# Three q, k turns of batch 2 by DMA transpose, an early gelu table, and a new order for batch 3's loads: a streaming-attention and gMLP kernel on one Trainium2 core

## The chip, the core and the metric

The kernel runs on one core of one Trainium2 chip. A time is device microseconds (us) of one execution; "the median" is over plain runs, and the profile is of one further execution, whose own time is given beside its span (first to last instruction of the program). The engines are named as in the profile: PE (TensorE), DVE (VectorE), ACT (ScalarE), POOL (GpSimd), SP (SyncE, which here only issues DMAs). Batches are counted from 0, so "batch 2" is the third and "batch 3" the fourth.

## The reference

Sliding-window attention with four sink tokens, then a gMLP block on the result. B = 4 batches, H = 8 heads, S = 768 tokens, head size 64; d_model = 512, d_ff = 1024.

```python
keep = is_sink | ((rel >= 0) & (rel < window))          # n_sink 4, window 128
a = softmax(where(keep, q @ k.T / sqrt(D), -1e9))
x = (a @ v).transpose(0, 2, 1, 3).reshape(B, S, 512)
h = gelu_tanh(x @ w_in)                                  # 512 -> 1024
u, v = h[..., :512], h[..., 512:]
v_n = (v - mean(v)) / sqrt(var(v) + 1e-6) * g_ln
v_s = einsum('ts,bsd->btd', w_sg, v_n) + b_sg[None, :, None]
out = x + (u * v_s) @ w_out
```

## The kernel before

All work is split into small steps, written by name in one long string, `STEPS` (from L20), and emitted in exactly that order. A step name is a function and its indices: `QK.2.0.1` is `QK(2, 0, 1)`. Each engine runs its own instructions in the order of the string, and each DMA is issued by the engine that owns its step: SP for transposes (`DQ`, `DK`, `XD`) and stores (`ST`), POOL for the loads that change f32 into bf16 (`LQ`, `LK`, `LVH`). So a step that waits holds back everything behind it on its engine, and the place of a step in the string sets its place in a queue.

For each batch the steps are these.

- `LQ`, `LK` (L225, L228) load 128 tokens of q or k, six each; `LVH` (L271) loads v for four heads, two each.
- q and k must stand with the head dimension on the partitions. For batches 0 to 2 this is done on PE: `TQ`, `TK` (`turns`, L361) put eight 128x128 transposes into one PSUM buffer, and `EQ`, `EK` (`turned`, L404; L197 and L198 are the copy itself) copy it to `qT`, `kT` on ACT (.A) or DVE (.D). For batch 3 it is done by `DQ`, `DK` (`by_dma`, L435), one DMA transpose on SP for the same eight blocks, with neither PE, PSUM nor a copy. One such step covers two tiles of 128 tokens: group 0, 1 or 2.
- `KS` takes the four sink keys, `SK` (L455) computes the sink scores of tokens 256 to 767 and `SX` (L462) their exponentials. `QK` computes window scores of a pair of heads p for two token tiles g, `EX` the exponentials (ACT), `MK` the masks (DVE or POOL), `AV` the product with v, `NR` the division.
- `XD` (L552) transposes the attention result by DMA, in two halves of three tiles. `MV` (L559, tiles 2g and 2g + 1) and `MU` (L600) are the first projection, `GV` (L566) and `GU` the gelu on ACT. `BN`, `RS` (L583, a power on POOL), `NM` and `Z` normalise.
- `SP` is the product over tokens (all six `Z` needed), `GT` and `GM` the gate, `OU` the second projection, `RA` the residual and `ST` the store.

PSUM is used through two rings: two wide buffers (`sc`) for `QK`, `MV` and `MU`, and four narrow ones (`mm`) for the rest. Two rings of two buffers hold `qT` and `kT`, so batch 2 writes where batch 0 was. The string overlaps batches: while the gate of batch b runs, attention of batch b + 1 or b + 2 runs between its steps. Exponentials and gelu need different tables on ACT; the first use of the other kind brings an ACT_TABLE_LOAD, which shows under the line of the activation that it serves.

The stretch that the change touches first: after the last exponentials of batch 2's group 0 (`EX.2.3.0`) and `OU.0.2`, PE does `TK.2.2`, `TQ.2.1`, `TQ.2.2`, then `MV.1.0`, `MU.1.0`, `MV.1.1`, `MV.1.2`, `MU.1.1`, `MU.1.2`, `OU.0.3`, `SK.2.0`, `QK.2.0.1`, `QK.2.1.1`, `OU.0.4`, `SP.1.0.0`. `MV.1.1` reuses the wide buffer of `MV.1.0`, which `GV.1.0` empties, and is the first to need the second half of `XD` (`XD.1.1`).

Of the kernel before, what the change touches and what calls it, by code (L numbers as in the profile page):

```python
# [28 lines left out]
MV.0.0 XE.0.1.A LK.1.2 NR.0.0.2 MK.0.3.2.D LK.1.3 NR.0.1.2 AV.0.2.2 AV.0.3.2 LQ.1.2 NR.0.2.2 GV.0.0 MV.0.1 NR.0.3.2
LQ.1.3 BN.0.0 LWS.1 XT.0.2 GV.0.1 MU.0.1 XE.0.2.A BN.0.1 WT.0 GU.0.1 TK.1.0 MV.0.2 RS.0.1 EK.1.0.A LK.1.4 NM.0.1  # L30
WE.0.A WT.1 GV.0.2 LK.1.5 TK.1.1 MU.0.2 LB.P EK.1.1.A BN.0.2 Z.0.0.A LK.2.0 WT.2 GU.0.2 MU.0.0 WE.1.D RS.0.2 WE.2.D
Z.0.1.A LQ.2.0 NM.0.2 Z.0.2.A Z.0.3.D Z.0.4.D WT.3 LQ.2.1 WT.4 GU.0.0 WE.3.D WT.5 LQ.1.4 Z.0.5.D TQ.1.1 QK.1.0.0
EQ.1.1.D QK.1.1.0 LQ.1.5 SP.0.0.0 WE.4.D LK.2.1 EX.1.0.0 VSM.1 SP.0.0.1 WE.5.D EX.1.1.0 LVH.1.0 GT.0.0.0 TK.1.2 KS.1
GT.0.0.1 QK.1.2.0 QK.1.3.0 EX.1.2.0 SP.0.0.2 LVH.1.1 GM.0.0.0.D EX.1.3.0 MK.1.2.0.D TQ.2.0 EK.1.2.A LQ.2.2 QK.1.0.1
EQ.2.0.D QK.1.1.1 TQ.1.2 EX.1.0.1 GT.0.0.2 LWO SP.0.0.3 EQ.1.2.D EX.1.1.1 LK.2.2 MK.1.0.1.D TK.2.0 MK.1.0.0.D QK.1.2.1
LK.2.3 EK.2.0.A QK.1.3.1 MK.1.3.0.D SK.1.0 GM.0.0.1.D LQ.2.3 SP.0.1.0 EX.1.2.1 GT.0.0.3 MK.1.1.0.D LQ.2.4 EX.1.3.1
SP.0.1.1 MK.1.1.1.D LQ.2.5 MK.1.2.1.D SX.1.0 QK.1.0.2 QK.1.1.2 GT.0.1.0 EX.1.0.2 GM.0.0.2.P SP.0.1.2 GT.0.1.1 EX.1.1.2
LK.2.4 GM.0.1.0.D AV.1.0.0 MK.1.3.1.D AV.1.1.0 LK.2.5 GM.0.0.3.D QK.1.2.2 GT.0.1.2 QK.1.3.2 EX.1.2.2 SP.0.1.3 NR.1.0.0
MK.1.1.2.P EX.1.3.2 NR.1.1.0 AV.1.2.0 AV.1.3.0 MK.1.0.2.P GT.0.1.3 QK.2.0.0 QK.2.1.0 NR.1.2.0 EX.2.0.0 OU.0.0
MK.1.2.2.P NR.1.3.0 TK.2.1 RA.0.0 AV.1.0.1 XD.1.0 EK.2.1.A MK.1.3.2.P AV.1.1.1 NR.1.0.1 AV.1.2.1 EX.2.1.0 GM.0.1.2.P  # L40
NR.1.1.1 AV.1.3.1 NR.1.2.1 QK.2.2.0 LK.3.0 QK.2.3.0 EX.2.2.0 OU.0.1 NR.1.3.1 GM.0.1.3.P EX.2.3.0 OU.0.2 XD.1.1 RA.0.1
GM.0.1.1.P TK.2.2 MK.2.3.0.D TQ.2.1 LVH.2.0 TQ.2.2 EQ.2.1.D MV.1.0 EQ.2.2.D LQ.3.0 EK.2.2.D LQ.3.1 VSM.2 MU.1.0 GV.1.0
MK.2.1.0.D LVH.2.1 BN.1.0 MV.1.1 GU.1.0 LQ.3.2 RA.0.2 LQ.3.3 MK.2.0.0.D MV.1.2 GV.1.1 MK.2.2.0.D LK.3.1 KS.2 LK.3.2
BN.1.1 MU.1.1 GV.1.2 LK.3.3 BN.1.2 RS.1.1 MU.1.2 GU.1.1 LQ.3.4 NM.1.1 Z.1.0.A RS.1.2 OU.0.3 GU.1.2 LQ.3.5 NM.1.2
Z.1.1.D SK.2.0 Z.1.4.D QK.2.0.1 Z.1.2.D Z.1.3.A QK.2.1.1 Z.1.5.D OU.0.4 RA.0.3 DK.3.0 SP.1.0.0 RA.0.4 SX.2.0 EX.2.0.1
SP.1.0.1 GT.1.0.0 DQ.3.0 EX.2.1.1 GM.1.0.0.D SP.1.1.0 MK.2.0.1.P GT.1.0.1 QK.2.2.1 ST.0.3 GT.1.1.0 QK.2.3.1 GM.1.0.1.P
DQ.3.1 EX.2.2.1 AV.2.0.0 SP.1.1.1 MK.2.1.1.D EX.2.3.1 MK.2.2.1.P NR.2.0.0 AV.2.1.0 QK.2.0.2 DQ.3.2 QK.2.1.2 KS.3
EX.2.0.2 MK.2.3.1.P NR.2.1.0 SP.1.1.2 GT.1.1.1 EX.2.1.2 OU.0.5 MK.2.0.2.P GT.1.1.2 ST.0.0 ST.0.4 QK.2.2.2 RA.0.5
QK.2.3.2 MK.2.1.2.P EX.2.2.2 AV.2.2.0 AV.2.3.0 NR.2.2.0 SP.1.1.3 EX.2.3.2 NR.2.3.0 QK.3.0.0 MK.2.3.2.P QK.3.1.0
GT.1.1.3 XD.2.0 EX.3.0.0 AV.2.0.1 MK.2.2.2.D AV.2.1.1 EX.3.1.0 NR.2.0.1 AV.2.2.1 GM.1.1.3.P ST.0.1 NR.2.1.1 AV.2.3.1  # L50
ST.0.2 ST.0.5 GM.1.1.0.P SK.3.0 NR.2.2.1 QK.3.2.0 QK.3.3.0 NR.2.3.1 EX.3.2.0 GM.1.1.2.P SP.1.0.2 EX.3.3.0 XD.2.1
SP.1.0.3 GT.1.0.2 SX.3.0 MK.3.3.0.D MV.2.0 GM.1.0.2.P DK.3.1 GM.1.1.1.D LK.3.4 MK.3.0.0.D OU.1.3 LVH.3.0 GV.2.0 OU.1.4
RA.1.3 LVH.3.1 OU.1.5 ST.1.3 RA.1.4 GT.1.0.3 MV.2.1 ST.1.4 MK.3.1.0.D LK.3.5 BN.2.0 GM.1.0.3.P MV.2.2 GV.2.1 BN.2.1
MU.2.1 GV.2.2 BN.2.2 RS.2.1 MU.2.0 GU.2.1 NM.2.1 RA.1.5 RS.2.2 MU.2.2 GU.2.0 NM.2.2 Z.2.4.D Z.2.5.D Z.2.0.A Z.2.1.D
OU.1.0 GU.2.2 Z.2.2.D MK.3.2.0.D OU.1.1 RA.1.0 Z.2.3.D QK.3.0.1 QK.3.1.1 RA.1.1 SP.2.0.0 EX.3.0.1 DK.3.2 EX.3.1.1
OU.1.2 MK.3.0.1.P GT.2.0.0 ST.1.5 VSM.3 ST.1.0 QK.3.2.1 ST.1.1 QK.3.3.1 EX.3.2.1 SP.2.1.0 GM.2.0.0.D MK.3.1.1.P RA.1.2
EX.3.3.1 SP.2.0.1 ST.1.2 MK.3.3.1.P QK.3.0.2 GT.2.0.1 QK.3.1.2 EX.3.0.2 SP.2.1.1 GT.2.1.0 MK.3.2.1.P EX.3.1.2
GM.2.1.0.D SP.2.1.2 GT.2.1.1 GM.2.0.1.D AV.3.0.0 MK.3.1.2.P GT.2.1.2 AV.3.1.0 NR.3.0.0 AV.3.2.0 AV.3.3.0 MK.3.0.2.P
NR.3.1.0 QK.3.2.2 QK.3.3.2 EX.3.2.2 SP.2.0.2 NR.3.2.0 NR.3.3.0 EX.3.3.2 SP.2.0.3 MK.3.2.2.P GT.2.0.2 XD.3.0 AV.3.0.1
GT.2.0.3 MK.3.3.2.P AV.3.1.1 NR.3.0.1 AV.3.2.1 GM.2.0.3.P NR.3.1.1 AV.3.3.1 SP.2.1.3 GM.2.0.2.D GM.2.1.1.P NR.3.2.1  # L60
OU.2.0 NR.3.3.1 GT.2.1.3 XD.3.1 OU.2.1 RA.2.0 GM.2.1.3.P OU.2.2 GM.2.1.2.D ST.2.0 RA.2.1 MV.3.0 RA.2.2 ST.2.1 OU.2.3
GV.3.0 OU.2.4 BN.3.0 MV.3.1 RA.2.3 RA.2.4 MV.3.2 ST.2.3 GV.3.1 ST.2.2 ST.2.4 BN.3.1 OU.2.5 GV.3.2 MU.3.2 BN.3.2 RS.3.1
MU.3.1 GU.3.2 NM.3.1 RS.3.2 NM.3.2 Z.3.0.D Z.3.1.A MU.3.0 Z.3.2.D Z.3.3.A Z.3.4.A Z.3.5.D RA.2.5 ST.2.5 SP.3.1.0
GU.3.0 SP.3.1.1 GU.3.1 GT.3.1.0 SP.3.1.2 GM.3.1.0.D GT.3.1.1 SP.3.1.3 GM.3.1.1.D GT.3.1.2 SP.3.0.0 GM.3.1.2.D SP.3.0.1
GT.3.0.0 GT.3.1.3 SP.3.0.2 GT.3.0.1 GM.3.1.3.P SP.3.0.3 GM.3.0.0.D GM.3.0.1.P GT.3.0.2 OU.3.3 GM.3.0.2.D GT.3.0.3
OU.3.4 GM.3.0.3.D RA.3.3 OU.3.0 RA.3.4 ST.3.3 OU.3.1 RA.3.0 ST.3.4 OU.3.2 ST.3.0 RA.3.1 OU.3.5 ST.3.1 RA.3.2 ST.3.2
RA.3.5 ST.3.5
"""


# [5 lines left out]
def kernel(  # L76
# [489 lines left out]
    def GV(b, g):  # L566
        return nc.scalar.activation(out=vt.new((b, g)), in_=sc_ring["v", b, g], func=AF.Gelu_apprx_tanh)  # L567
# [4 lines left out]
    def BN(b, g):
        mv = mvs.get(b)
        sts = [tiny.tile([128, 6], F32, name=f"st{jl}") for jl in range(2)]
        for jl in range(2):
            nc.vector.bn_stats(out=sts[jl], in_=vt[b, g][:, jl, :])  # L576
        for jl in range(2):
            nc.vector.bn_aggr(out=mv[:, 2 * g + jl, :], in_=sts[jl])
        if g:
            nc.vector.tensor_scalar(out=rs.get(b)[:, part(g)], in0=mv[:, part(g), 1], scalar1=1e-6,  # L580
                                    scalar2=None, op0=ALU.add)

    def RS(b, g):  # L583
        r = rs[b][:, part(g)]
        nc.gpsimd.tensor_tensor(r, r, neg_half[:, part(g)], op=ALU.pow)  # L585
# [127 lines left out]
```

## Time and profile before

| | |
|---|---|
| median of 3 runs | 157.62 us (157.57 to 157.83) |
| the profiled execution | 156.68 us, of it span 155.0 us |
| granted TensorE clock over the span | 0.997 |
| busy: PE / DVE / POOL / ACT | 93% / 79% / 64% / 64% of the span |
| DMA queue of POOL's loads (q0) | 64608 packets, 11.01 MB |
| DMA queue of SP's DMAs (q1) | 21544 packets, 13.41 MB |
| one DMA transpose of 128x1024 (`DQ`, `DK`), issue to landing | 3.0 to 4.4 us |
| eight PE transposes, start to start of one | 0.056 us |
| the copy of 128x1024 behind them on DVE | 0.68 us |
| ACT_TABLE_LOAD | 1.28 us |

How to read it: an engine's share is the mean over the span, and PE is the engine that is nearly always at work. A group's line gives its count, its busy time and the idle time before it with the one that ended that idle time. A timeline line gives start and length in us, engine, line, operation, out<-in, and in brackets the idle time of that engine just before. "PEld" is PE's weight load, which overlaps its matmuls. A q behind an engine's name marks its queue of DMA issues.

### The profile page before, as it was taken

Reading aid. Unit: us, or ns where it says so; the run is one execution under the profiler, and the core shown is the slowest. Engines: PE = TensorE matmul, PEld = TensorE weight load, DVE = VectorE, ACT = ScalarE, POOL = GpSimd, SP = SyncE. Lnnn points to the kernel's source line nnn. Section 1 sums busy time; section 2 is a strip of 40 time slices with the busy share of each in tenths; the row PEclk is TensorE's granted clock in tenths of the full one; section 3 lists DMA queues with packets and bytes.
Section 4 is the critical chain, followed back from the end, with each engine's and each line's share of the span. In section 5 each row is a group of like instructions: output and inputs, shape, how many; then the busy total and the mean of one; then the engine's idle time right before and its main releaser. Section 6 shows DMA issues by size and latency. Waiting matters only on the chain.

```text
span 155.0 us, 3736 instructions
## 1 busy us (share of the span) xinstructions
PE 144.0 (93%) x1483; PEld 93.5 (60%) x1495; DVE 122.9 (79%) x295; ACT 98.9 (64%) x110; POOL 99.9 (64%) x127
## 2 busy tenths in 40 slices
PE   6697799999999989989999999999999999999990
...
GB/s 162 261 367 162 149 194 210 166 194 218 147 149 153 181 159 135 153 152 156 153 255 138 140 270 179 177 190 80 217 68 24 82 237 4 203 68 2 0 237 171
DMA packets 86169, 24.65 MB, mean 159 GB/s; under 512 B 78660, under 2 KB 83016, under 8 KB 86152
## 3 DMA queue, kind: packets, MB, share of 16 engines
q0 software_dynamic: 64608, 11.01, 96.1%
q1 hardware_dynamic: 21544, 13.41, 33.6%
...
## 4 chain that ended last, share of the span: by engine, by line
PE 59%; DMA 15%; POOL 10%; DVE 7%; issue 4%; ACT 2%; SPq 1%; ACTq 0%; POOLq 0%
PE mm L624 15%; PE mm L641 12%; DMA v_sb<-in_v_dram 11%; PE sc L563 10%; PE sc L604 8%; PE sc L480 4%; DMA uT<-in_k_dram 4%; PE mm L521 3%; POOL q L223 3%; DVE st L576 2%; PE mm L525 2%; POOL P L495 2%; PE mm L528 2%; POOL P L498 2%; DVE P L492 1%
## 5 line engine op out<-in xcount | busy, mean ns | idle before, releaser
L485 ACT ACTIVATE P<-sc 128x1024 bf16<-128x1024 f32 (+1 forms) x48 | 43.5, 956 | 10.0 <-PE sc L480 9.9
L624 PE MATMUL mm<-wsgT,z 128*128 128x384 bf16 x192 | 34.1, 327 | 0.0
L624 PEld LDWEIGHTS <-z 128*128 128x128 bf16 x192 | 17.7, 98 | 11.9 <-issue 0.7
L563 PE MATMUL sc<-w_in_sb,xT 128*128 128x512 bf16 x92 | 21.8, 379 | 0.9 <-ACT vt L567 0.7
L629 DVE SCALAR_TENSOR_TENSOR gtmp<-mm,g_sb,b_bc 128x384 bf16<-128x384 f32 x32 | 19.2, 612 | 4.2 <-PE mm L624 3.6
L641 PE MATMUL mm<-w_out_sb,wsg_gated 128*128 128x512 bf16 x89 | 22.0, 379 | 0.3
L604 PE MATMUL sc<-xT,w_in_sb 128*128 128x256 bf16 x192 | 22.1, 273 | 0.0
L634 POOL TENSOR_TENSOR wsg_gated<-gtmp,uT 128x384 bf16<-128x384 bf16 x15 | 14.9, 1004 | 10.9 <-DVE gtmp L629 10.9
L576 DVE BATCH_NORM_STATS2 st<-vt 128x6 f32<-128x512 f32 x24 | 15.4, 685 | 7.5 <-ACT vt L567 7.4
L495 POOL TENSOR_SCALAR_AFFINE_SELECT P<-P 128x512 bf16<-128x512 bf16 x21 | 14.1, 669 | 11.3 <-ACT P L485 11.0
L604 PEld LDWEIGHTS <-w_in_sb 128*128 128x128 bf16 x192 | 18.6, 98 | 3.0
L538 DVE TENSOR_TENSOR x_sb<-mm,rcp 128x384 bf16<-128x384 f32 (+1 forms) x36 | 18.5, 513 | 1.2
L567 ACT ACTIVATE vt<-sc 128x1024 f32<-128x1024 f32 x12 | 12.3, 1028 | 9.0 <-PE sc L563 8.9
L645 DVE TENSOR_TENSOR ot<-mm,x_sb 128x512 f32<-128x512 f32 x24 | 16.1, 684 | 2.3 <-PE mm L641 2.2
L585 POOL TENSOR_TENSOR rs<-rs,neg_half 128x4 f32<-128x4 f32 (+1 forms) x8 | 7.0, 869 | 16.5 <-DVE rs L580 15.1
L223 POOL DMA_DIRECT2D k<-in_k_dram x18 | 16.4, 924 | 1.2 <-DMA v_sb<-in_v_dram 1.2
L521 PE MATMUL mm<-v_sb,P 128*128 128x65 bf16 x192 | 16.3, 194 | 0.7 <-DVE x_sb L538 0.4
L223 POOL DMA_DIRECT2D q<-in_q_dram x18 | 16.7, 949 | 0.0
L521 PEld LDWEIGHTS <-P 128*128 128x128 bf16 x192 | 14.6, 97 | 2.7 <-issue 0.6
L525 PE MATMUL mm<-v_sb,P 128*128 128x65 bf16 x160 | 15.5, 194 | 0.4 <-POOL P L498 0.4
L563 PEld LDWEIGHTS <-xT 128*128 128x128 bf16 x96 | 9.2, 98 | 10.9 <-issue 0.9
L480 PE MATMUL sc<-qT,kT 64*128 64x128 bf16 (+1 forms) x256 | 14.8, 238 | 1.0 <-DVE qT L198 0.6
...
## 6 DMA issues: line engine op xcount, KB each, us to landing
...
```

The source lines that it names most:

```text
L223: return nc.gpsimd.dma_start(out=dst.rearrange("p (h d) -> p h d", h=H), in_=heads(src, b, i))
L480: nc.tensor.matmul(sc[:, hl, c:c + 128 * ni], at(kT, b)[rows, j, p, :], at(qT, b)[rows, i:i + ni, p, :], start=not biased, stop=(not biase ...
L485: nc.scalar.activation(out=P.new((b, p, g))[:, :, 0:w], in_=sc_ring[b, p, g][:, :, 0:w], func=AF.Exp, scale=scale)
L521: nc.tensor.matmul(av[:, il, hl, :], pt[:, hl, c:c + 128], vb[:, h, i, :], start=first, stop=False)
L525: nc.tensor.matmul(av[:, il, hl, :], pt[:, hl, c:c + 128], vb[:, h, i - 1, :], start=False, stop=(i < 2 and il == n - 1 and hl == 1))
L538: nc.vector.tensor_mul(x_sb.get(b)[:, i0:i0 + n, 128 * p:128 * (p + 1)].rearrange("p t (h d) -> p t h d", h=2), av[:, :, :, 0:Dh], rcp[:, ...
L563: nc.tensor.matmul(hp[:, jl, :], xT[b][:, 2 * g + jl, c, :], w_in_sb[:, c, d_half:2 * d_half], start=(c == 0), stop=(c == KD - 1))
L576: nc.vector.bn_stats(out=sts[jl], in_=vt[b, g][:, jl, :])
L604: nc.tensor.matmul(hp[:, dc // 2, 256 * (dc % 2):256 * (dc % 2 + 1)], w_in_sb[:, c, 128 * dc:128 * (dc + 1)], xT[b][:, 2 * g:2 * g + 2, c, :],
L624: nc.tensor.matmul(ps[:, 0:NH], z[b][:, si, 128 * dc:128 * (dc + 1)], wsgT[:, si, NH * hf:NH * (hf + 1)], start=(si == 0), stop=(si == NT ...
L629: nc.vector.scalar_tensor_tensor(out=gtmp.new((b, hf, dc)), in0=mm_ring["g", b, hf, dc][:, 0:NH], scalar=g_sb[:, dc:dc + 1], in1=b_bc[:, N ...
L641: nc.tensor.matmul(ps, gated(b, hf)[:, dc, 128 * tl:128 * (tl + 1)], w_out_sb[:, dc, :], start=(dc == 0), stop=(dc == KU - 1))
```

## The change

Four edits, three of them in the string alone.

1. `TK.2.2`, `TQ.2.1`, `TQ.2.2` and their copies `EQ.2.1.D`, `EQ.2.2.D`, `EK.2.2.D` are taken out. `DQ.2.1`, `DQ.2.2`, `DK.2.2` are put in, on SP directly behind `XD.1.1`. Group 0 of q and groups 0 and 1 of k of batch 2 stay on PE.
2. A new step `TL`, one gelu of a 128x1 tile into an unused tile, stands on ACT between `EX.2.3.0` and `GV.1.0`.
3. On POOL, the loads of batch 3 are reordered: `LK.3.1` moves up ahead of `LVH.2.1`; `LK.3.2` and `LK.3.3` move from ahead of `RS.1.1` to behind `RS.1.2`, and `LQ.3.5` follows `RS.1.2` directly, ahead of them.
4. `SK.3.0` moves on PE from ahead of `QK.3.2.0` to behind `QK.3.1.1`, `SX.3.0` on ACT from behind `EX.3.3.0` to behind `EX.3.1.1`.

The lines of the string are broken anew in the diff, so it is shown here step by step, + and - at the places of the steps; the new function is whole.

```diff
 EX.2.3.0
+TL
 OU.0.2 XD.1.1
+DQ.2.1 DQ.2.2 DK.2.2
 RA.0.1 GM.0.1.1.P
-TK.2.2
 MK.2.3.0.D
-TQ.2.1
 LVH.2.0
-TQ.2.2 EQ.2.1.D
 MV.1.0
-EQ.2.2.D
 LQ.3.0
-EK.2.2.D
 LQ.3.1
+LK.3.1
 VSM.2 MU.1.0 GV.1.0 MK.2.1.0.D LVH.2.1 BN.1.0 MV.1.1 GU.1.0 LQ.3.2 RA.0.2 LQ.3.3 MK.2.0.0.D MV.1.2 GV.1.1 MK.2.2.0.D
-LK.3.1
 KS.2
-LK.3.2
 BN.1.1 MU.1.1 GV.1.2
-LK.3.3
 BN.1.2 RS.1.1
+LQ.3.4
 MU.1.2 GU.1.1
-LQ.3.4
 NM.1.1 Z.1.0.A RS.1.2
+LQ.3.5 LK.3.2 LK.3.3
 OU.0.3 GU.1.2
-LQ.3.5
 NM.1.2 Z.1.1.D SK.2.0
...
 GM.1.1.0.P
-SK.3.0
 NR.2.2.1 QK.3.2.0 QK.3.3.0 NR.2.3.1 EX.3.2.0 GM.1.1.2.P SP.1.0.2 EX.3.3.0 XD.2.1 SP.1.0.3 GT.1.0.2
-SX.3.0
 MK.3.3.0.D MV.2.0
...
 QK.3.0.1 QK.3.1.1
+SK.3.0
 RA.1.1 SP.2.0.0 EX.3.0.1 DK.3.2 EX.3.1.1
+SX.3.0
 OU.1.2
...
+    spare = sb.tile([128, 1], F32, name="spare")
...
+    def TL():
+        return nc.scalar.activation(out=spare, in_=neg_half[:, 0:1], func=AF.Gelu_apprx_tanh)
```

More of the change, by code (lines that the diff above doesn't have):

```diff
@@ L29 @@
[L29 to L67, printed above, removed]
+QK.0.2.1 EX.0.2.0 LK.1.0 KS.0 VSM.0 SK.0.2 EX.0.2.1 SK.0.1 MK.0.2.0.D AV.0.0.0 LW.1 QK.0.3.0.1 MK.0.1.0.D SX.0.1 SX.0.2
+QK.0.3.1 MK.0.2.1.P GCP.D NR.0.0.0 EX.0.3.0 AV.0.0.1 AV.0.1.0 AV.0.1.1 NR.0.0.1 EX.0.3.1 QK.0.1.2 NR.0.1.0 AV.0.2.0
@@ new lines @@
+AV.0.3.0 EX.0.1.2 MK.0.3.1.P NR.0.1.1 QK.0.2.2 AV.0.2.1 NR.0.2.0 EX.0.2.2 TQ.1.0 NR.0.3.0 MK.0.1.2.P QK.0.3.2 AV.0.3.1
+EQ.1.0.A NR.0.2.1 XT.0.0 NR.0.3.1 LWS.0 AV.0.0.2 EX.0.3.2 AV.0.1.2 XE.0.0.D LK.1.1 XT.0.1 MK.0.2.2.D MV.0.0 XE.0.1.A
+LK.1.2 NR.0.0.2 MK.0.3.2.D LK.1.3 NR.0.1.2 AV.0.2.2 AV.0.3.2 LQ.1.2 NR.0.2.2 GV.0.0 MV.0.1 NR.0.3.2 LQ.1.3 BN.0.0 LWS.1
+XT.0.2 GV.0.1 MU.0.1 XE.0.2.A BN.0.1 WT.0 GU.0.1 TK.1.0 MV.0.2 RS.0.1 EK.1.0.A LK.1.4 NM.0.1 WE.0.A WT.1 GV.0.2 LK.1.5
+TK.1.1 MU.0.2 LB.P EK.1.1.A BN.0.2 Z.0.0.A LK.2.0 WT.2 GU.0.2 MU.0.0 WE.1.D RS.0.2 WE.2.D Z.0.1.A LQ.2.0 NM.0.2 Z.0.2.A
@@ new lines @@
+Z.0.3.D Z.0.4.D WT.3 LQ.2.1 WT.4 GU.0.0 WE.3.D WT.5 LQ.1.4 Z.0.5.D TQ.1.1 QK.1.0.0 EQ.1.1.D QK.1.1.0 LQ.1.5 SP.0.0.0
+WE.4.D LK.2.1 EX.1.0.0 VSM.1 SP.0.0.1 WE.5.D EX.1.1.0 LVH.1.0 GT.0.0.0 TK.1.2 KS.1 GT.0.0.1 QK.1.2.0 QK.1.3.0 EX.1.2.0
+SP.0.0.2 LVH.1.1 GM.0.0.0.D EX.1.3.0 MK.1.2.0.D TQ.2.0 EK.1.2.A LQ.2.2 QK.1.0.1 EQ.2.0.D QK.1.1.1 TQ.1.2 EX.1.0.1
+GT.0.0.2 LWO SP.0.0.3 EQ.1.2.D EX.1.1.1 LK.2.2 MK.1.0.1.D TK.2.0 MK.1.0.0.D QK.1.2.1 LK.2.3 EK.2.0.A QK.1.3.1
+MK.1.3.0.D SK.1.0 GM.0.0.1.D LQ.2.3 SP.0.1.0 EX.1.2.1 GT.0.0.3 MK.1.1.0.D LQ.2.4 EX.1.3.1 SP.0.1.1 MK.1.1.1.D LQ.2.5
@@ new lines @@
+MK.1.2.1.D SX.1.0 QK.1.0.2 QK.1.1.2 GT.0.1.0 EX.1.0.2 GM.0.0.2.P SP.0.1.2 GT.0.1.1 EX.1.1.2 LK.2.4 GM.0.1.0.D AV.1.0.0
+MK.1.3.1.D AV.1.1.0 LK.2.5 GM.0.0.3.D QK.1.2.2 GT.0.1.2 QK.1.3.2 EX.1.2.2 SP.0.1.3 NR.1.0.0 MK.1.1.2.P EX.1.3.2
+NR.1.1.0 AV.1.2.0 AV.1.3.0 MK.1.0.2.P GT.0.1.3 QK.2.0.0 QK.2.1.0 NR.1.2.0 EX.2.0.0 OU.0.0 MK.1.2.2.P NR.1.3.0 TK.2.1
+RA.0.0 AV.1.0.1 XD.1.0 EK.2.1.A MK.1.3.2.P AV.1.1.1 NR.1.0.1 AV.1.2.1 EX.2.1.0 GM.0.1.2.P NR.1.1.1 AV.1.3.1 NR.1.2.1
+QK.2.2.0 LK.3.0 QK.2.3.0 EX.2.2.0 OU.0.1 NR.1.3.1 GM.0.1.3.P EX.2.3.0 TL OU.0.2 XD.1.1 DQ.2.1 DQ.2.2 DK.2.2 RA.0.1
```

31 lines of the change are left out of this document (26 added, 5 removed).

## The prediction

> **What bounds the kernel now.** I read the page's shares first, then PE's waits, then the timeline where the change sits, then the queues there.
>
> ```profile
> PE 144.0 (93%) x1483; PEld 93.5 (60%) x1495; DVE 122.9 (79%) x295; ACT 98.9 (64%) x110; POOL 99.9 (64%) x127
> ...
> PE   6697799999999989989999999999999999999990
> ```
>
> PE is busy in nearly every slice from the fifth on. Asked for PE's waits between 62 and 150 us, the profile has one group:
>
> ```profile
> PE sc L563 <- ACT vt L567: 0.7, 1, 0.7
> ```
>
> So between 62 us and the last stores the time is PE's own work, plus one stall of 0.7 us. A change gains there what it takes off PE, as long as no new wait appears. The stall, in the timeline:
>
> ```profile
> 61.02 0.61 PE L379 MATMUL mm<-iden,k 128*128 128x128 bf16 x8
> ...
> 61.46 1.06 PE L379 MATMUL mm<-iden,q 128*128 128x128 bf16 x16
> ...
> 62.36 1.89 PE L563 MATMUL sc<-w_in_sb,xT 128*128 128x512 bf16 x8
> ...
> 64.08 1.91 PE L604 MATMUL sc<-xT,w_in_sb 128*128 128x256 bf16 x16
> 64.33 1.28 ACT L567 ACT_TABLE_LOAD   x1 [3.59 <-PE sc L563]
> ...
> 65.62 1.02 ACT L567 ACTIVATE vt<-sc 128x1024 f32<-128x1024 f32 x1
> ...
> 66.70 0.38 PE L563 MATMUL sc<-w_in_sb,xT 128*128 128x512 bf16 x1 [0.70 <-ACT vt L567]
> ```
>
> The 24 transposes, MV.1.0, MU.1.0; then PE waits for GV.1.0, which itself stood behind a table load. ACT had been idle for 3.59 us.
>
> **Part 1, turns by DMA.** PE: the 24 transposes go, MV.1.0 starts at 61.02 instead of 62.36: 1.34 us, all on the path. DVE: three copies go (0.69 + 0.69 + 0.68 us), worth nothing directly, since DVE next idled 1.62 us for GV.1.0. MV.1.0 needs XD.1.0, issued at 55.55; with the 4.8 us of XD.1.1 it lands at 60.4, in time.
>
> **Part 2, the table.** TL's load can start when EX.2.3.0 ends (59.22 + 1.51 = 60.73) and ends at 62.01. TL itself has no row; it lies between nothing and the 0.60 us of the 128x512 SX.2.0, so it is done by 62.6 at the latest. I take 0.2; all of it is inside the idle 3.59 us. MV.1.0 now ends at 62.91 (its modelled end 64.25 less 1.34), GV.1.0 runs 62.95 to 63.97. PE could start MV.1.1 when MU.1.0 is issued: its last matmul started at 65.72, plus one spacing of 0.11, less 1.34: 64.49. GV.1.0 is then no longer last. **Next late is XD.1.1**: issued at 59.83, 4.8 us to landing, so 64.65 to 64.7. MV.1.1 starts at 64.72 instead of 66.70: **1.98 us** (1.34 + 0.87 from start to start, less 0.23 for XD.1.1). Without TL, GV.1.0 would end at 65.21 and the gain be 1.4. XD.1.1 could only be later than before by the DMAs put in behind it in the same queue, 0 to 0.3; I take 0, as DQ.2.1 is issued at 61.38 and XD.1.1's packets are nearly through when its own begin.
>
> **Part 3, POOL's order.** The gain must get past POOL's power step, RS.1.1, on which Z and SP.1.0.0 hang.
>
> ```profile
> 62.23 1.47 POOL L272 DMA_DIRECT2D v_sb<-in_v_dram  x1
> 63.70 1.76 POOL L223 DMA_DIRECT2D q<-in_q_dram  x2
> 65.43 1.44 POOL L272 DMA_DIRECT2D v_sb<-in_v_dram  x1
> 66.83 1.79 POOL L223 DMA_DIRECT2D q<-in_q_dram  x2
> 68.57 2.67 POOL L223 DMA_DIRECT2D k<-in_k_dram  x3
> 71.53 1.03 POOL L585 TENSOR_TENSOR rs<-rs,neg_half 128x4 f32<-128x4 f32 x1 [0.29 <-DVE rs L580]
> ```
>
> The loads start when GM.0.1.1 ends and don't move. RS.1.1's input is ready at 71.46 now and at 69.48 after. In the old order POOL is free at 71.24, and only 0.29 us of the gain would pass. Two issues of 0.87 us fewer ahead of it make POOL free at 69.50: it meets the input within 0.02. Then RS.1.1, LQ.3.4, RS.1.2 follow at 69.5, 70.55, 71.5, as before less 2.0; LQ.3.5, LK.3.2, LK.3.3 end near 75.1, and POOL's next work, MK.2.0.1, comes at 78.95 - 1.98 = 77.0. Added wait: POOL once waited 1.16 us at 51.76 for the landing of the load eight issues before. By that count LQ.3.5 waits for LVH.2.0 and LK.3.3 for LQ.3.1; nothing but MK.2.0.1 is behind them, with 1.9 us to spare.
>
> **Part 4, sink scores.** PE's work is the same: 0.33 us (89.71 to 90.05) leaves the place before QK.3.2.0 and comes back before SP.2.0.0 at 107.82. PE has no wait at either place, so the bounds are 0.33 gained and 0.33 lost; I take 0. SX.3.0 (0.61) leaves the place before the table load at 92.53, where GV.2.0 waits for PE anyway (0.56), and comes ahead of EX.3.2.1, where ACT was idle 0.28 and EX.3.0.1 now starts 0.33 sooner.
>
> **What the transposes cost the queues.** This is the unknown. XD.1.1 beside loads, and loads alone (packets in 61.5 to 64.2, and in 64.5 to 76.5):
>
> ```profile
> q1 hardware_dynamic: 1568, 0.39, 83.5%
> q0 software_dynamic: 773, 0.10, 56.2%
> ```
>
> ```profile
> q0 software_dynamic: 14120, 1.79, 235.7%
> ```
>
> A 128x1536 transpose is 1568 packets, so a 128x1024 one is 1045. Loads alone run 1177 packets a us; beside loads a transpose got 581 a us here, and 252 at worst (504 between 57.5 and 59.5, beside 1036 of loads). DQ.2.1 and DQ.2.2 are 2090 packets from about 64.2: done after 3.6 to 8.3 us, landed 0.4 later, at 68.2 to 72.9. SK.2.0 needs them at 74.60 - 1.98 = 72.62; DK.2.2 is needed by QK.2.0.2 at 80.0. The nearer row is XD.1.1's, so I take no loss; the worst costs 0.3.
>
> The other side: loads lose time. At XD.1.1's mix, 2.7 us held 773 / 1177 = 0.66 us of loads, so 1568 transpose packets cost 2.04 us, 768 a us. Three cost 4.1 us, all on the loads of v and of batch 3. Readers: LVH.2.0 landed at 69.0 and is needed at 78.2; LVH.2.1 at 73.1, needed at 83. LQ.3.5 (78.71) rises two loads in the queue (1.7 us), and loses 4.1 plus up to 2.7 for DK.3.0 and DQ.3.0, which ran after the loads before and now run beside them: at most 83.8; played through in order, 82.6. On SP, DQ.3.2 waits for it, and behind DQ.3.2 stand two stores and XD.2.0; the three took 3.27 us (80.65 to 83.92). XD.2.0 took 3.72 us to land and MV.2.0 needs it at 92.44 - 1.98 - 0.33 = 90.13, so LQ.3.5 may land until 83.1. In time by 0.5, or late by up to 0.7 (with the 252 rate, over 1). I take in time.
>
> A rule speaks against the change: the Trainium skill, "VectorE: DVE Perf Modes", section Rules for kernel authors, would turn 128x128 on TensorE if PSUM will do, and its section on the three transpose paths puts a block at 390 ns there and 1309 ns by DMA. Taken as a price per block, eight blocks would need 10.5 us, and SK.2.0 would come some 8 us later than before (an estimate from that page of the Trainium skill). The trace speaks otherwise: eight blocks landed in 3.0 to 4.4 us, and PE spent 0.056 us a block.
>
> **The sum.** 1.34 + 0.87 - 0.23 = 1.98 us, less 0.08 for the meetings without slack (XD.1.1, RS.1.1): 1.9. The profiled execution, 156.68 us with span 155.0, becomes 154.8 with span 153.1. It ran 0.94 us under the median; the same 1.9 off the median of 157.62 is 155.7.
>
> **Rivals.**
>
> - *As summed*: 155.7, own range 155.3 to 156.1. 58%.
> - *More*: XD.1.1 early and SK.3.0's 0.33 us kept: 2.2 + 0.3, 155.1. 4%.
> - *SP's queue late*: XD.2.0 behind DQ.3.2, or DQ.2.2 by a little, gives 0.4 to 1.3 back: about 156.5. For it: SP is in order, and loads fill the engines from 64.5 to 76.5. Against: the 0.5 us computed. 22%.
> - *The gain doesn't pass*: POOL or DVE holds Z, SP.1.0.0 waits, and RS.1.1 stays near 71.5: 157.4. Against: POOL's free time computed above. 6%.
> - *Slower*: in the full load queue the transposes get far less than XD.1.1 did. It decides at 203 packets a us, where DQ.2.2 lands at 74.9 and SK.2.0 is later than before. At two thirds of the worst stretch, 168, it lands at 77.0: 2.4 us late, 160.0. For it: the worst stretch came as the loads ran out, here they don't. Against: 581 beside LK.3.0. 9%.
> - *Transposes one at a time*: each starts only when the one before has landed, and each is stretched as in the worst mix. Alone a transpose ran 709 packets a us (1064 between 59.5 and 61.0), so 4.4 us becomes 4.4 x 709 / 252 = 12.4, and DQ.2.2 lands at 61.4 + 24.8 = 86.2, 11.6 later than SK.2.0 runs now: 169. Against: DK.3.0 and DQ.3.0, issued 1.33 us apart, landed 0.9 apart. 1%. It is the case in which the order of the Trainium skill, "VectorE: DVE Perf Modes", section Rules for kernel authors, would be right here.
>
> Faster by over 0.2% (0.3 us, about what a measurement of this kernel can tell from none): 84%; within 6%; slower 10%. The range 155.2 to 157.0 takes in the sum, the late queue and a part of "more".
>
> **What would show it.** Right: no transposes in 61 to 62.4, a table load at 60.7 under TL's line, MV.1.1 at 64.7 released by XD.1.1, RS.1.1 at 69.5, no PE wait at SK.2.0, MV.2.0 at 90.1 to 90.5, every later step 1.9 earlier. Wrong: a PE wait ended by a DMA at SK.2.0 or MV.2.0, a POOL wait at LK.3.2, or a wait of PE on z.

## The result, and the profile after

The changed kernel is slower. Its median of four runs is 160.94 us (159.31 to 163.73), that of before beside it 157.59 us; the ratio is **1.0127, 95% interval 1.0079 to 1.0175**. Medians here hold all runs, and ratios leave out executions over 1.5% above the fastest of their kernel (two of after's four; those that the profiles of e1 and e12 show are such too), so the two need not agree. The profiled execution of after took 159.31 us, its span 157.6 us, against 156.68 and 155.0. Forecast were 155.7 us and a span of 153.1.

From the page of after: busy shares, the granted clock by slices, SP's DMA queue. Line numbers from L567 on stand three higher than before.

```profile
PE 145.4 (92%) x1471; PEld 92.9 (59%) x1471; DVE 121.8 (77%) x292; ACT 99.2 (63%) x111; POOL 100.0 (63%) x127
...
PEclk9999999999999999999999599999999999999999
...
q1 hardware_dynamic: 24712, 14.19, 38.6%
```

PE has fewer instructions and yet more busy time: in one slice, near 88 us, it ran at half clock. SP's queue has 3168 packets more, the three transposes. PE's waits between 62 and 150 us (total, times, longest):

```profile
PE mm L521 <- DVE gtmp L632: 2.5, 1, 2.5
PE sc L563 <- DMA xT<-x_sb: 0.2, 1, 0.2
```

The stall for GV.1.0 is gone, and a longer one has come that the prediction doesn't have. Where the time went is read best from the same step in both profiles. Start of an ACT step after, less its start before:

| step | shift, us | what lies between |
|---|---|---|
| EX.2.3.0 | +0.52 | before the change's first step: drift of this execution |
| GV.1.1 | -1.28 | parts 1 and 2: **1.80 gained** |
| EX.2.2.1 | -1.03 | 0.25 lost at SP.1.0.0 |
| EX.2.3.2 | -1.08 | |
| EX.3.0.0 | +2.96 | **4.04 lost** between 84 and 90 us |
| EX.3.1.1 | +2.50 | 0.46 regained ahead of QK.3.2.0, of it 0.33 from SK.3.0's old place |
| EX.3.2.1 to the end | +2.83 | 0.33, SK.3.0 in its new place |

The timeline of after where the gain is made (start, length, ..., idle before):

```profile
61.27 1.28 ACT L570 ACT_TABLE_LOAD   x1
...
61.93 1.90 PE L563 MATMUL sc<-w_in_sb,xT 128*128 128x512 bf16 x8 [0.23 <-DMA xT<-x_sb]
...
63.92 1.02 ACT L567 ACTIVATE vt<-sc 128x1024 f32<-128x1024 f32 x1 [1.16 <-PE sc L563]
...
65.41 3.62 PE L563 MATMUL sc<-w_in_sb,xT 128*128 128x512 bf16 x16
```

No transposes, the table ahead of GV.1.0, MV.1.1 directly behind MU.1.0. And where it is lost, on DVE, PE and SP's queue, the same steps of DVE and SP in before first, then after:

```profile
82.22 0.52 DVE L447 TENSOR_TENSOR ks_sink<-kT,halfsel 128x32 bf16<-128x32 bf16 x1
...
75.15 1.23 SPq L437 DMA_TRANSPOSE kT<-k  x1
...
79.20 3.61 SPq L437 DMA_TRANSPOSE qT<-q  x2
...
87.08 1.42 SPq L554 DMA_TRANSPOSE xT<-x_sb  x1
```

```profile
84.62 0.58 DVE L447 TENSOR_TENSOR ks_sink<-kT,halfsel 128x32 bf16<-128x32 bf16 x1 [3.40 <-DMA kT<-k]
...
86.47 0.25 PE L521 MATMUL mm<-v_sb,P 128*128 128x65 bf16 x3 [2.49 <-DVE gtmp L632]
...
76.94 1.24 SPq L437 DMA_TRANSPOSE kT<-k  x1
...
82.82 5.78 SPq L437 DMA_TRANSPOSE qT<-q  x2
...
89.80 1.52 SPq L554 DMA_TRANSPOSE xT<-x_sb  x1
```

KS.3 on DVE waits 3.40 us for DK.3.0; in before it waited for nothing. Behind it in DVE's order stand a division and the gate step GT.1.1.1 (L632), which empties the narrow PSUM buffer that AV.2.2.0 needs, so PE stops there for 2.49 us. Then the clock is 0.5 from 86.76 us for 3.41 us. On SP, the issues of DQ.3.1 and DQ.3.2 take 5.78 us (3.61 before), and XD.2.0 comes at 89.80 instead of 87.08. DK.3.0 took 7.65 us from issue to landing (76.94 to 84.60); before, 4.40.

Why it took so long shows in the packets. The two queues between 77 and 80 us, with the DMAs issued there, and then between 82 and 86 us:

```profile
DMA packets 3574, 0.45 MB, mean 151 GB/s; under 512 B 3574, under 2 KB 3574, under 8 KB 3574
...
q0 software_dynamic: 3574, 0.45, 300.9%
...
kT<-k SPq DMA_TRANSPOSE x1
qT<-q SPq DMA_TRANSPOSE x1
```

```profile
DMA packets 3312, 0.64 MB, mean 160 GB/s; under 512 B 3311, under 2 KB 3311, under 8 KB 3311
...
q0 software_dynamic: 1656, 0.21, 79.5%
q1 hardware_dynamic: 1655, 0.42, 79.3%
```

In the first stretch DK.3.0 and DQ.3.0 are issued and not one of their packets runs: the loads alone move 1191 a us. DK.3.0's first packet comes at 81.3 us, 4.3 us after its issue. In the second stretch both queues move the same count, 414 a us each. A transpose's packet holds twice the bytes of a load's (0.42 MB in 1655 against 0.21 MB in 1656). So in bytes the engines move no less than with loads alone, 160 GB/s for 151, and one packet of a transpose takes the place of two of the loads. The Trainium skill, "DMA: Bandwidth & Descriptors", section Queues, rings and completion order, says that each DMA engine goes round the queues that have work, one packet from each; the equal counts agree, as far as the profile's packets are the ones meant. But DQ.2.2's packets, beside the loads between 66.5 and 70.5 us of after, do not come in equal counts:

```profile
DMA packets 3736, 0.62 MB, mean 154 GB/s; under 512 B 3735, under 2 KB 3735, under 8 KB 3735
...
q0 software_dynamic: 2694, 0.34, 210.1%
q1 hardware_dynamic: 1041, 0.26, 53.3%
```

Here the loads move 674 and the transposes 260 a us. What holds in all three stretches is the sum of the bytes, 151 to 160 GB/s.

### The profile page after: what moved, and what is told of

Its sections match the earlier page's. It is cut to its first block, busy times and chain, and to the rows that moved or that the text cites. A ratio compares the mean times of both kernels' runs of the same rounds, so it can differ in the third digit from the quotient of the medians.

```text
span 157.6 us, 3707 instructions
## 1 busy us (share of the span) xinstructions
PE 145.4 (92%) x1471; PEld 92.9 (59%) x1471; DVE 121.8 (77%) x292; ACT 99.2 (63%) x111; POOL 100.0 (63%) x127
## 4 chain that ended last, share of the span: by engine, by line
PE 61%; DMA 29%; ACT 3%; POOL 2%; DVE 2%; issue 1%; SPq 1%
PE mm L627 15%; PE sc L563 11%; PE sc L607 10%; PE mm L644 10%; DMA k<-in_k_dram 6%; DMA qT<-q 5%; DMA v_sb<-in_v_dram 5%; DMA kT<-k 5%; DMA uT<-in_k_dram 4%; DMA xT<-x_sb 4%; PE sc L480 3%; PE mm L521 3%; PE mm L525 2%; PE mm L528 2%; PE mm L379 2%; PE mm L619 1%
## 5 line engine op out<-in xcount | busy, mean ns | idle before, releaser
L627 PE MATMUL mm<-wsgT,z 128*128 128x384 bf16 x192 | 35.2, 333 | 0.1
L632 DVE SCALAR_TENSOR_TENSOR gtmp<-mm,g_sb,b_bc 128x384 bf16<-128x384 f32 x32 | 19.1, 610 | 4.9 <-PE mm L627 4.8
L644 PE MATMUL mm<-w_out_sb,wsg_gated 128*128 128x512 bf16 x96 | 22.7, 379 | 0.0
L567 ACT ACTIVATE vt<-sc 128x1024 f32<-128x1024 f32 x12 | 12.3, 1026 | 10.2 <-PE sc L563 10.2
```

The costliest lines, as they stand in the source:

```text
L627: nc.tensor.matmul(ps[:, 0:NH], z[b][:, si, 128 * dc:128 * (dc + 1)], wsgT[:, si, NH * hf:NH * (hf + 1)], start=(si == 0), stop=(si == NT ...
L632: nc.vector.scalar_tensor_tensor(out=gtmp.new((b, hf, dc)), in0=mm_ring["g", b, hf, dc][:, 0:NH], scalar=g_sb[:, dc:dc + 1], in1=b_bc[:, N ...
L644: nc.tensor.matmul(ps, gated(b, hf)[:, dc, 128 * tl:128 * (tl + 1)], w_out_sb[:, dc, :], start=(dc == 0), stop=(dc == KU - 1))
```

## Experiments

The letters of the theories are those of each expectation. Kernels measured together shared the runs of before; its median was 157.32 (e1 to e4), 156.84 (e5 to e8), 157.65 (e9 to e12) and 156.85 us (e13 to e15).

| run | median, us | ratio to before, 95% |
|---|---|---|
| e1 KS.3 late | 160.54 | 1.0105 [1.0070, 1.0141] |
| e2 KS.3 late, XD.2.0 first | 161.39 | 1.0148 [1.0094, 1.0201] |
| e3 PE filled | 159.50 | 1.0131 [1.0078, 1.0185] |
| e4 turns on PE | 156.84 | 0.9978 [0.9944, 1.0013] |
| e5 one turn | 155.57 | **0.9934 [0.9892, 0.9975]** |
| e6 turns alone | 158.68 | 1.0120 [1.0048, 1.0191] |
| e7 table alone | 156.43 | 0.9961 [0.9917, 1.0005] |
| e8 loads deferred | 157.42 | 1.0069 [1.0027, 1.0111] |
| e9 deferred again | 157.86 | 1.0048 [0.9990, 1.0106] |
| e10 two turns | 158.99 | 1.0106 [1.0041, 1.0171] |
| e11 one deferred | 157.95 | 1.0052 [0.9990, 1.0113] |
| e12 turns added | 161.95 | 1.0181 [1.0085, 1.0277] |
| e13 deferred, clear | 158.15 | 1.0068 [1.0022, 1.0115] |
| e14 one deferred, clear | 160.35 | 1.0202 [1.0148, 1.0256] |
| e15 v beside Z | 158.90 | 1.0122 [1.0076, 1.0167] |

### Is it the one wait at KS.3? (e1, e2, e3)

e1, against after:

```diff
-KS.3
 EX.2.0.2
...
 MK.3.0.0.D
+KS.3
```

> The changed kernel with KS.3 (sink keys of batch 3, DVE) moved behind MK.3.0.0.D, some 12 us later; its only reader, SK.3.0, still comes later. Theory A: the loss is KS.3 waiting on DVE for the landing of DK.3.0 (84.6 us), which holds back DVE, then PE, then PE's clock. Then DVE's 3.4 us and PE's 2.5 us of idle time at 84 to 86.5 us are gone and the clock stays at 1. Under A alone the time is that of before less 1.0 to 1.4: about 156.4, ratio 0.992. Rival B, SP's queue: XD.2.0 still stands behind DQ.3.1 and DQ.3.2, which SP finished issuing only at 88.6, so it goes out near 89.8 and lands near 93.5, while MV.2.0 is due near 91.0: PE waits 2 to 2.5 us there, and the time is 158 to 159.5. Rival C, the loads as such are late (v of batch 2): AV.2.2.0 waits for a load and little is gained.

KS.3 waits no more, and the time stays (the intervals of e1 and after overlap): PE now waits 1.9 us at QK.3.0.0 for DQ.3.0 and 2.4 us at MV.2.0 for XD.2.0, in an execution of 162.08 us (the shortest of e1 took 158.66). Rival B's wait came; that KS.3's place alone is the cause fell.

e2, e1 and besides:

```diff
-DQ.3.1
...
-DQ.3.2
...
 XD.2.0
+DQ.3.1 DQ.3.2
```

> As the kernel with KS.3 late, and XD.2.0 put ahead of DQ.3.1 and DQ.3.2 on SP (the two go behind it). Theory A with rival B: both waits gone, XD.2.0 goes out at 86, lands near 90, MV.2.0 waits less than 0.3: 156.0 to 156.5, ratio 0.990 to 0.993. If B is wrong, the same time as with KS.3 late alone. If the transposes beside loads hurt in other ways (v late, QK.3.0.0 waiting for DQ.3.0), 157 or more, with a PE wait ended by a DMA.

XD.2.0 is in time (MV.2.0 waits for nothing). DQ.3.0 is not, as PE's waits of e2 say:

```profile
PE sc L480 <- DMA qT<-q: 2.7, 1, 2.7
```

The clock is 0.5 again, from 88.03 us for 3.41 us.

e3, against after: ten matmuls without use, to keep PE at work through the wait.

```diff
+HM.10
 QK.2.3.2
```

> The changed kernel with ten matmuls of 512 columns on constant data, overwritten afterwards, ahead of QK.2.3.2: 2.15 us of PE work in the place of most of PE's idle 2.5 us; KS.3's wait stays. It takes PE's idle time away and leaves the wait. Theory A with the clock as a second price: PE resumes at 86.5 as before, but at full clock, the slice at half clock is gone, and 1.0 to 1.4 us come back: about 158.2. If the half clock is not due to the idle time, or costs nothing, the time stays at 159.4 or gets worse by the delay of EX.2.3.2 (up to 2.1 us).

No half clock, and less lost up to EX.3.0.0: 2.59 us from EX.2.0.2 (-1.83 to +0.76), 4.04 in after. But to the end it is 4.63 (+2.80), in after 3.91. PE's waits of e3:

```profile
PE sc L563 <- DMA xT<-x_sb: 1.9, 2, 1.7
PE sc L480 <- DMA qT<-q: 0.2, 1, 0.2
```

So the half clock at KS.3's wait does not set the total. Two executions of after say the same: 159.74 us with a mean clock of 1.000, 159.31 us with 0.989. Whatever one reader is spared, the next one in SP's queue takes: DK.3.0, DQ.3.0, DQ.3.1, DQ.3.2, XD.2.0 are late as a row.

### Which part? (e4, e6, e7, e12)

e4: after, with the three turns on PE and DVE as before (parts 2, 3, 4 alone).

> The changed kernel with the three turns back on PE (parts 2, 3 and 4 of the change alone). TL takes the table load off the path: MV.1.1 can start when MU.1.0 has been issued, 0.87 us earlier than before; PE's 0.7 us wait is gone: 156.8 to 157.0, ratio 0.995. Theory A: KS.3 waits little or nothing, since DK.3.0 has no other transposes ahead of it (landing by 81.5). Rival D: the new order of loads alone brings DK.3.0 beside the loads and makes KS.3 wait here too, 1 us or more: slower than before.

The table is worth 0.87 us at GV.1.1 (+0.99 to +0.12), as forecast; 0.52 are lost again at SP.1.0.0. DK.3.0 lands at 77.34 and nobody waits for it. Parts 2 to 4 don't make the loss.

e6: before, with part 1 alone.

> The kernel before with part 1 alone: the three turns by DMA, no TL, the old order of the loads, SK.3.0 in its old place. Theory A: the loss is the transposes' own and does not need the new order. In the old order LK.3.1 stands behind LVH.2.1 and three q loads; it landed at 75.0 and comes at 78 to 80, so DK.3.0 lands at 85 to 88 and KS.3 or QK.3.0.0 waits 2 us or more, while part 1 by itself gains at most 1.3: 159.5 to 163. Rival C (the new order of the loads is what makes the transposes late): no wait over 0.5 us, 156.3 to 157.6.

The same in the old order of the loads: LK.3.1 lands at 80.83 (75.01 before; the drift at EX.2.3.0 is 1.46), KS.3 waits 1.92 us and MV.2.0 1.5. The shift falls to +0.52 at GV.1.1 and ends at +3.51. The median, 158.68 us, is less than the 159.5 to 163 expected. The new order is not what makes the transposes late.

e7: before, with `TL` behind `EX.2.3.0`.

> The kernel before with TL alone. Up to GV.1.1 0.87 us are gained, as in the run with parts 2 to 4. With POOL's old order RS.1.1 can come only 0.29 us sooner, since POOL is issuing loads until 71.24. If SP.1.0.0 has 0.6 us to spare behind the Z steps, all 0.87 is kept: 156.4 to 156.8. If it has none, 0.3 is kept: 157.0 to 157.4, with a PE wait for z.

GV.1.1 comes 0.46 sooner in this execution (+0.37 to -0.09; MV.1.0 waited 0.18 for XD.1.0), Z.1.0 0.75, and 0.62 are kept to the end, more than POOL's old order was thought to let through. The interval takes in no change.

e12: before, with the three transposes put in and nothing taken out.

```diff
 XD.1.1
+DX.q.1 DX.q.2 DX.k.2
...
+    def DX(w, g):
+        src = q16 if w == "q" else k16
+        n = {("q", 1): 0, ("q", 2): 1, ("k", 2): 2}[w, g]
+        return nc.sync.dma_start_transpose(out=extra[:, n, :].rearrange("p (a i) -> p a i", i=128),
+                                           in_=src[2][:, 2 * d_model * g:2 * d_model * (g + 1)])
```

> The price of the three transposes by themselves: the kernel before, all its PE turns and copies kept, with three more DMA transposes behind XD.1.1, of the same blocks of q and k as in the change, into a tile that nobody reads (its space is that of an unused ring). Nothing else is changed, and what they write is not used. Theory A: all loss is in the queues; LK.3.1, landed at 75.0 before, lands near 79, DK.3.0 after 84, and KS.3, QK.3.0.0 or MV.2.0 wait: 158.3 to 160.5, less than with the turns taken off PE only in as much as PE comes later to the same readers. Rival E (the loss comes from what was taken off PE and DVE, or from the wait of a reader of the turned blocks): within 0.3 us of before, 156.5 to 157.2.

The profile is of an execution of 161.77 us (the shortest of e12 took 159.37). Its drift is 0.20. LK.3.1 lands at 80.48, DK.3.0 is issued at 80.61, KS.3 waits 3.48 us. The three transposes alone cost 1.8%, with a wide interval, and no reader of theirs can be the cause, since there is none.

### How many? (e5, e10)

e5, against after; e10 is the same without the two lines of TQ.2.2.

```diff
 DQ.2.1
-DQ.2.2 DK.2.2
 RA.0.1 GM.0.1.1.P
+TK.2.2
 MK.2.3.0.D LVH.2.0
+TQ.2.2
 MV.1.0
+EQ.2.2.D
 LQ.3.0
+EK.2.2.D
```

> The changed kernel, but with only DQ.2.1 by DMA; TQ.2.2, TK.2.2 and their copies are back on PE and DVE. Theory A (loads and transposes share the 16 DMA engines, each queue gets some 410 packets a us while both are full, so every transpose put in makes the loads and the transposes behind them late by its own packets, and the time is lost only when a reader is met): one transpose costs the loads about 1.4 us instead of 4.1, LK.3.1 lands near 74 instead of 76.8, DK.3.0 near 81, KS.3 waits under 0.5 us; 8 transposes are still off PE (0.45 us): 156.3 to 157.3. Rival B (any transpose that is put into the full load queue blocks SP's queue, whatever their number): KS.3, QK.3.0.0 or MV.2.0 still wait over 1.5 us: 158.5 to 160.

> The changed kernel with two of the three turns by DMA (DQ.2.1, DQ.2.2); TK.2.2 and its copy are back on PE and DVE. The third point between one turn (ratio 0.9934) and three (1.0127). Theory A: LK.3.1 landed at 71.5 with one turn and at 76.8 with three, so near 74 here; DK.3.0 near 81 to 82, XD.2.0 issued near 87.5; a small wait at KS.3 or MV.2.0, and 16 transposes off PE: 156 to 158. Rival B (a step from none to all, by whether DQ.2.2 is caught in the full load queue): as with three turns, 158.5 to 160.

Times in us, less each run's shift at EX.2.3.0 (+0.99, -0.16, +0.20, +0.52):

| turns by DMA | LK.3.1 landed | DK.3.0 issued | KS.3 waits | XD.2.0 issued | ratio |
|---|---|---|---|---|---|
| 0 (e4) | 71.00 | 71.16 | 0 | 86.68 | 0.9978 |
| 1 (e5) | 71.70 | 71.85 | 0 | 86.23 | 0.9934 |
| 2 (e10) | 74.72 | 74.86 | 1.0 | 88.08 | 1.0106 |
| 3 (after) | 76.28 | 76.42 | 3.4 | 89.28 | 1.0127 |

PE's only wait of e5 between 62 and 150 us:

```profile
PE mm L628 <- DVE ot L649: 0.3, 1, 0.3
```

The landings go up with each turn; the time goes down first, since 8 transposes are off PE and no reader is met, and then up by 1.7% in one step. By its time e10 is rival B's case (158.99 us in 158.5 to 160); LK.3.1 landed at 74.92, near theory A's 74. The landings grow at every turn, by 0.7, 3.0 and 1.6 us, and the time jumps where they first meet readers. The first turn cost the loads less than theory A had it (LK.3.1 at 71.54, expected near 74). From none to three LK.3.1 comes 5.28 us later; 3168 transpose packets, each in the place of two load packets, would be 6336 / 1191 = 5.3 us. In e10 the readers are met: 0.51 us are lost at QK.3.0.0, 2.02 at MV.2.0 (a wait of 1.8 for XD.2.0), 0.39 at MV.2.1. **e5 is the one version whose whole interval lies below 1.** That its single turn adds to parts 2 to 4 is read from the profiles alone: from EX.2.3.0 to the end e5 gains 0.85 us and e4 0.41, but the intervals of e5 and of e4 and e7 overlap.

### Loads out of the way (e8, e9, e11, e13, e14)

e8, against after:

```diff
-LQ.3.4
...
-LQ.3.5 LK.3.2 LK.3.3
...
-DQ.3.1
...
-DQ.3.2
...
 XD.2.0
+DQ.3.1
...
 GM.1.0.2.P
+LK.3.2 LK.3.3 LQ.3.4 LQ.3.5
...
 ST.1.4
+DK.3.1 DQ.3.2
```

(KS.3 is behind MK.3.0.0, GM.1.0.3, LK.3.4, LK.3.5, LVH.3.0 behind GT.1.0.3, LVH.3.1 behind RS.2.2.)

> The changed kernel with its three DMA turns, but nothing that is not needed yet in their way: LK.3.2, LK.3.3, LQ.3.4, LQ.3.5 are issued behind GM.1.0.2 (near 93) instead of at 71 to 76, DQ.3.1 behind XD.2.0, DK.3.1 and DQ.3.2 behind ST.1.4, KS.3 behind MK.3.0.0. Theory A: with the loads through by 80.5 and two transposes fewer in the queue, DK.3.0 and DQ.3.0 land by 83.5, XD.2.0 is issued as soon as its input is there, and no PE wait over 0.5 us is left between 70 and 95: the 1.8 us gained by GV.1.1 are kept but for what POOL's later gates cost: 155.3 to 156.3. Rival D (the three transposes of batch 2 alone are enough to make DK.3.0 and DQ.3.0 late, whatever comes behind them): QK.3.0.0 still waits over 1.5 us: 158 to 160.

Between 70 and 90 us PE waits for nothing over 0.5 us, and from EX.2.3.0 (+0.75) to EX.3.2.0 (-1.63) 2.38 us are gained, 0.34 of them from SK.3.0's old place: with the loads gone the three transposes cost nothing there. KS.3, DQ.3.1 and DQ.3.2 are moved too, so the run to compare is e2, which has them late as well and the loads in their way, and waits 2.7 us at QK.3.0.0. The rival fell. After 89 us it is given back: XD.2.0 and XD.2.1 late beside DQ.3.1 (1.25 up to GV.2.1), SK.3.0 waiting 0.96 for DQ.3.2, and its move (0.33).

e9 puts DQ.3.1 behind XD.2.1, SK.3.0 behind QK.3.3.1, and LVH.3.0, LVH.3.1 behind RS.2.2.

> The changed kernel with its three DMA turns and the loads deferred, and with what was late in the run before this one put right: DQ.3.1 behind XD.2.1 instead of ahead of it, both loads of v for batch 3 behind RS.2.2, so that DK.3.1, DQ.3.2 and DK.3.2 meet fewer loads, and SK.3.0, SX.3.0 behind QK.3.3.1 and EX.3.3.1. If theory A holds (the loss is only the meeting of transposes and loads, 2.38 us were gained from EX.2.3.0 to EX.3.2.0 in the run with the loads deferred, and the rest was given back at XD.2.1 and at SK.3.0), some 2 us are kept to the end: 154.6 to 155.6 beside a before of 156.8. Rival: the loads that are moved have to run somewhere, and the meeting only moves to 92 to 108, to XD.2.1, DK.3.1 or DK.3.2: one wait of 0.5 to 1.5 us there, 156 to 157.

2.48 us are gained up to EX.3.1.1 (+1.56 to -0.92), and 1.23 lost at one step, SP.2.0.0, which waits for Z: a loss of this order itself, see e15. Then 0.33 go at SK.3.0 and 0.68 at AV.3, where PE resumes at 116.92, right behind the landing of LVH.3.1 at 116.87. e11 is e9 with one turn.

> The run with one turn by DMA, with loads, SP's order and sink scores as in the second version with deferred loads. One turn alone waited for no DMA, so deferring has only the 0.53 us to give that the Z steps on DVE lost beside POOL's load issues (EX.2.2.1 came out at -0.95 instead of -1.48). Theory A: 155.2 to 156.0, and slower than three turns with deferred loads by the 0.9 us of the 16 transposes on PE. Rival: the same as one turn alone, 155.6.

The same 1.23 at SP.2.0.0 and 0.83 more where v lands at 115.81, late for AV.3: deferring costs one turn more than it can give.

e13 issues behind GM.1.0.2 in the order LK.3.2, LK.3.3, LQ.3.5, LK.3.4, LK.3.5, GM.1.0.3, LVH.3.0, LVH.3.1, and only then RS.2.1; e14 is that with one turn.

> Three turns by DMA, loads deferred, SP's order and sink scores as in the second version with deferred loads, but behind GM.1.0.2 POOL issues LK.3.2, LK.3.3, LQ.3.5, LK.3.4, LK.3.5, then GM.1.0.3, LVH.3.0, LVH.3.1, and only then RS.2.1, so that no load is issued beside a Z step; LQ.3.4 stays at 71. If the two causes (transposes beside loads, and load issues beside Z) are all there is, the Z steps at 103 take 1.91 us for four, EX.3.2.1 is at the shift of EX.3.1.1 plus 0.33 (SK.3.0), and 2.0 to 2.2 us are kept to the end against the kernel before: ratio 0.985 to 0.99. Rival (the moved loads cost the same wherever they run): a wait for DMA of 0.5 us or more at QK.3.0.1, QK.3.0.2 or AV.3.0.0, and ratio 0.997 to 1.005.

> The same with one turn by DMA (TQ.2.2 and TK.2.2 on PE). The 16 transposes are back on PE, 0.9 us: if the two causes are all, ratio 0.990 to 0.994, slower than three turns in the same order. Rival: the same ratio as the three turns or better, if the two further transposes still cost their 0.9 us in the queues.

Z is back at 1.92 us, and the rival's waits come (the ratio, 1.0068, is a little above its 1.005): the meeting has moved. DK.3.1, issued at 98.07 beside the loads of v, lands at 106.29 (8.2 us), DQ.3.2 after 11.3. PE in e13's timeline:

```profile
106.34 0.61 PE L480 MATMUL sc<-qT,kT 64*128 64x256 bf16 x12 [1.06 <-DMA kT<-k]
...
110.75 0.40 PE L459 MATMUL mm<-qT,ks_sink 128*32 128x512 bf16 x4 [1.30 <-DMA qT<-q]
...
114.48 0.62 PE L480 MATMUL sc<-qT,kT 64*128 64x256 bf16 x12 [1.27 <-DMA kT<-k]
```

Of the 2.23 us gained by EX.3.2.0 (+0.17 to -2.06) nothing is left at the end (+2.10), and e14, with a wait of 2.1 us and 3.41 us of half clock behind it, has the highest ratio of all. All five runs were slower than theory A had them, by 1.1 us or more, and no order was found in which three turns pay.

### What slows Z? (e15)

e15, against before:

```diff
-LVH.3.0
...
-LVH.3.1
...
 RS.2.2
+LVH.3.0 LVH.3.1
```

> The kernel before, with LVH.3.0 and LVH.3.1 moved on POOL from 94 to 97 to behind RS.2.2, beside the Z steps of batch 2, and nothing else. If a load issue on POOL slows Z on DVE: four Z take 3.7 to 3.8 us instead of 1.92, PE waits about 1 us for z at SP.2.0.0, and the time goes up by 1.0 to 1.9 us (some of it perhaps by v landing late at AV.3.0.0): ratio 1.006 to 1.012. Rival (Z was slow for another reason, by what the deferred order did to DVE): four Z take under 2.2 us and the ratio is within 0.3% of 1.

The four Z of batch 2 on DVE in before, then in e15, with PE's wait there:

```profile
104.19 1.92 DVE L597 TENSOR_SCALAR z<-vt,rs,nmr 128x512 bf16<-128x512 f32 x4
```

```profile
103.99 3.81 DVE L597 TENSOR_SCALAR z<-vt,rs,nmr 128x512 bf16<-128x512 f32 x4
```

```profile
PE mm L624 <- DVE z L597: 1.1, 1, 1.1
```

Nothing else was changed, the shift goes from -0.20 to +1.08 at that step, and stays. A load that POOL issues beside Z makes Z longer: 1.91 us with none, 2.16 with one (before, at 74.36), 2.75 with three (after), 3.03 (e4), 3.81 with two of v. The data under way does not do it: in e13 both loads of v were still to land (at 108.16 and 113.17) while four Z took 1.92. The Trainium skill, "SBUF — State Buffer", section Who interferes with whom, has POOL and some DVE modes shut each other out from a port pair that they share, whichever comes first keeping it; the longer Z agrees, though no run here shows the port itself.

## Why the prediction was wrong, point by point

- **Part 1 and 2, right.** 1.80 us at GV.1.1 for 1.98 forecast. Table load at 61.27, TL 0.20 us, MV.1.1 behind MU.1.0. e4 shows TL's 0.87 by itself. The part that is missing lies ahead of MV.1.0, which waited 0.23 us for XD.1.0: that was taken to land 4.8 us after its issue and took 5.9.
- **Part 3, wrong by 0.25 to 0.5 us.** RS.1.1 did run at 70.25, 1.28 earlier. "Nothing but MK.2.0.1" is behind the loads moved on POOL, but the Z steps of DVE run beside their issue: 2.75 us for 2.16. The step priced what is queued behind the issues, not what runs beside them.
- **Part 4, right.** It was taken as 0 between 0.33 gained and 0.33 lost, and both came: 0.46 are regained ahead of QK.3.2.0 in after (0.35 in e4), and 0.33 are lost between EX.3.1.1 and EX.3.2.1.
- **The queues: the step that failed.** It is the list of **readers**. The list followed LQ.3.5 to DQ.3.2 and XD.2.0, and noted that DK.3.0 and DQ.3.0 "now run beside them", but charged that to the loads alone. Their own landing was never worked out, and their readers KS.3, on DVE, and QK.3.0.0 are not on the list. Before, DK.3.0 landed at 79.55 and KS.3 came at 82.22: 2.67 us to spare. After, DK.3.0 was issued 1.79 us later and took 3.25 us longer, and KS.3 came 1.00 us sooner: 1.79 + 3.25 + 1.00 - 2.67 = 3.37 us, and the wait is 3.40. Behind it 4.04 us are lost.
- **The price of the transposes.** XD.1.1's stretch gave 768 transpose packets a us of the loads' time, 4.1 us for three. With the load queue full a transpose packet costs two of the loads', and LK.3.1 came 5.28 us later with three turns than with none. LQ.3.5 was still to land at 82.6 to 83.8 and landed at 83.05; that is in part luck, since DK.3.0 and DQ.3.0, which were to cost it up to 2.7 us, had no packet before 81.27.
- **The rate.** 581 packets a us were taken as what a transpose gets beside loads, and 252 were the worst case. DQ.2.2 got 260, near the worst, and landed at 72.98, the late end of its range (68.2 to 72.9). SK.2.0 ran at 73.31 and did not wait: no loss, as forecast, but by 0.3 us. Between 82 and 86 us the transposes got 414. The late start of DK.3.0 is not in any rate.
- **The rivals.** "SP's queue late" gave 156.5; its mechanism came, by another reader and with another size. In the profile of after MV.2.0 does not wait for XD.2.0; it does in e1, e3 and e10. The 0.5 us to spare for XD.2.0 was computed from LQ.3.5's landing, but DQ.3.2 was issued at 84.94, behind DQ.3.0 and DQ.3.1, whose issues are held 3.73 and 1.95 us. The slower rival named DQ.2.2, which was in time. "One at a time", 169, fell: DQ.2.2 landed at 72.98, not 86.2. The packets of DQ.2.2 and DK.2.2 did run one behind the other (from 66.3 and from 71.8 us), but DK.2.2's began before DQ.2.2 had landed.
- **What was not counted.** That a 2.5 us wait of PE is followed by half clock. It makes KS.3's wait dear, but e3 shows that it does not set the total.

What stays open: what holds DK.3.0's first packet. It is not the number of loads ahead of it that have not landed: with seven of them in after it waited 4.33 us, with six in e10 4.27, with four in e5 and e14 4.26, but with four in before 1.99 and with three in e4 2.66. No run tells what sets it.
